# The first of two expert mixtures: sums kept in PSUM, weight splits moved to other steps, two output tiles interleaved

## The chip, the core and the metric

One core of a Trainium2 chip runs the whole program. Its engines work side by side and meet through semaphores: TensorE (PE in the profile, with its weight loads as PEld), VectorE (DVE), ScalarE (ACT), GpSimd (POOL), and SyncE (SP), whose queue issues most DMA transfers. TensorE writes its results into PSUM; everything else lies in SBUF. The metric is the device time of one execution in microseconds, lower is better.

## The reference

Attention with a cluster mask gives 1536 rows of 512 numbers. A first mixture of experts gives each row to exactly one of 8 experts, 192 rows to each. A second mixture runs all rows through all 4 experts and adds the results with given weights.

```python
def _moe_ref(x, w_gate, w1, w2):                 # x (1536, 512), 8 experts, F = 1024
    cap = N // E                                 # 192 rows per expert
    ...
    for e in range(E):
        mask = assigned == e
        h = np.maximum(x[mask] @ w1[e], 0.0)     # layer 1: 512 -> 1024
        out[mask] = h @ w2[e]                    # layer 2: 1024 -> 512

def _moe2_ref(x, domain_probs, w1, w2):          # 4 experts, every row through each
    for e in range(E):
        h = np.maximum(x @ w1[e], 0.0)
        out += p[:, e:e + 1] * (h @ w2[e])
```

## The kernel before

The program has four parts, one after the other: attention, routing (which rows belong to which expert), the first mixture and the second. All of the change lies in the function `moe`, nearly all of it in the first mixture. The order of the instructions on each engine is the order in which the code writes them; nothing reorders them.

**Numbers in halves.** Products are taken in a reduced fp32 format. So each operand is held as a high part and a low part (the rest), and the product is the sum of high times high, high times low and low times high. For weights, `split(l, e, i)` makes one chunk of 128x1024 of layer `l`, expert `e`: ScalarE copies `raw` to `hi` (line L1025), then GpSimd (first mixture, `i` even) or VectorE (all others) computes `lo = raw - hi` (L1026), and the next chunk's load goes to SP's queue. Each layer of an expert has four chunks. The pools `wp` hold four chunks of each kind, the ring of loaded chunks eight.

**One expert of the first mixture.** Its 192 rows lie transposed, high and low part beside each other, in `X1`. Layer 1 makes eight tiles `f`, each from four pairs of matmuls (L1129 with 384 columns: high and low rows times high weights; L1130 with 192 columns: high rows times low weights, added into the first half). Then come the transposes of the rows of a later expert (`fetch`, L1072), then layer 2 makes four tiles `i`, each from eight pairs (L1143, L1144) that read `h[:, k]`, the eight results of layer 1. A tile is one PSUM buffer `p` of a pool of six (name `p1`) and has two halves `p[:, 0]` and `p[:, 1]` that must be added.

**The join of a tile.** ScalarE copies the second half to SBUF (`r`, L1099), VectorE adds it to the first (`t`, L1100). One tile later (`later`, `flush`) ScalarE makes the high part from `t` (`h` or `XH`, L1104) and VectorE the low part (`h` at L1106, `XL` at L1108), which reads `t` and the high part. The last tile of layer 1 is joined to its end at once.

**Where the splits stand before.** In layer 1: for the first expert the last two chunks of its own layer 2 (tiles 0 and 1); for all, chunk 0 and 1 of the next expert's layer 1 behind tiles 3 and 5. In layer 2: two chunks each behind tiles 0 and 1, one each behind tiles 2 and 3.

**The second mixture** takes 512 rows at a time, layer 1 in eight tiles (L1164 to L1166), layer 2 in four (L1186 to L1188), with its own splits behind every second tile of some blocks.

Of the kernel before, what the change touches and what calls it, by code (L numbers as in the profile page):

```python
# [27 lines left out]
F32 = mybir.dt.float32  # L28
# [949 lines left out]
def moe(ctx, tc, xd, idx, w1, w2, u1, u2, out, idf, idb, route):  # L978

    nc = tc.nc  # L980
# [4 lines left out]
    cap = N // E1  # L985
    KD, KF = D // 128, F // 128
# [5 lines left out]
    XH = big.tile([128, KD, N], F32R, name="XH")  # L992
    XL = big.tile([128, KD, N], F32R, name="XL")
# [4 lines left out]
    for e in range(E1):  # L998
        a = w1[e].rearrange("(k p) f -> p k f", p=128)
        b = w2[e].rearrange("(k p) d -> p k d", p=128)  # L1000
        chunks += [(1, e, i, a[:, :, i * 256:(i + 1) * 256]) for i in range(4)]
        chunks += [(2, e, i, b[:, :, i * 128:(i + 1) * 128]) for i in range(4)]
    for e in range(E2):
        a = u1[e].rearrange("(k p) f -> p k f", p=128)
        b = u2[e].rearrange("(k p) d -> p k d", p=128)
        chunks += [(1, E1 + e, i, a[:, :, i * 256:(i + 1) * 256]) for i in range(4)]
        chunks += [(2, E1 + e, i, b[:, 2 * i:2 * i + 2, :]) for i in range(4)]
    raw, HI, LO, nload = {}, {}, {}, [0]

    def load():  # L1010
        if nload[0] < len(chunks):
            l, e, i, ap = chunks[nload[0]]
            t = ring.tile([128, 1024], F32, name="raw")
            nc.sync.dma_start(t.rearrange("p (a b) -> p a b", a=ap.shape[1]), ap)
            raw[l, e, i] = t
            nload[0] += 1

    def split(l, e, i, sub=None):

        if e == E1 + E2:  # L1020
            return
        w = raw.pop((l, e, i))
        hi = wp.tile([128, 1024], F32R, name=f"hi{l}")
        lo = wp.tile([128, 1024], F32R, name=f"lo{l}")
        nc.scalar.activation(hi, w, AF.Copy)  # L1025
        (sub or (nc.gpsimd if e < E1 and i % 2 == 0 else nc.vector)).tensor_sub(lo, w, hi)  # L1026
        HI[l, e, i], LO[l, e, i] = hi, lo
        load()
# [9 lines left out]
    with ExitStack() as mc:  # L1038
        xgp = mc.enter_context(tc.tile_pool(name="xgp", bufs=4))

        def gather(j):
            if j not in XG:
                XG[j] = xgp.tile([128, D + E2], F32, name="xg")
            nc.gpsimd.indirect_dma_start(out=XG[j], out_offset=None, in_=xd,
                                         in_offset=bass.IndirectOffsetOnAxis(ap=idx[:, j:j + 1], axis=0))

        def first_rows():
            for j in range(4):
                gather(j)

        route(first_rows, ahead)
        m1 = mc.enter_context(tc.tile_pool(name="m1", bufs=1))
        m2 = mc.enter_context(tc.tile_pool(name="m1b", bufs=2))
        pg = ctx.enter_context(tc.tile_pool(name="pg", bufs=6, space=bass.MemoryType.PSUM))
        pxt = ctx.enter_context(tc.tile_pool(name="pxt", bufs=2, space=bass.MemoryType.PSUM))


        wt = pg.tile([128, 4, 128], F32, name="p1")
        for _ in range(WARM):
            nc.tensor.matmul(wt, idb, idb[:, None, :].to_broadcast([128, 4, 128]), start=True, stop=True)  # L1060

        def xpose(j):

            x = XG.pop(j)
            parts = 2 if j < 2 else 1
            K = KD // parts
            ps = []
            for i in range(parts):
                p = (pg if parts > 1 else pxt).tile([128, K, 128], F32, name="p1" if parts > 1 else "px")
                for k in range(K):  # L1070
                    o = (i * K + k) * 128
                    nc.tensor.transpose(p[:, k], x[:, o:o + 128], idf)  # L1072
                ps.append(p)
            s = j * 128
            while s < (j + 1) * 128:
                e = s // cap
                z = min((e + 1) * cap, (j + 1) * 128)
                if e not in X1:
                    X1[e] = m1.tile([128, KD, 2, cap], F32R, name="X1", bufs=3)
                d = slice(s - e * cap, z - e * cap)  # L1080
                c = slice(s - j * 128, z - j * 128)
                for i, p in enumerate(ps):
                    t = X1[e][:, i * K:i * K + K]
                    nc.scalar.activation(t[:, :, 0, d], p[:, :, c], AF.Copy)
                    nc.vector.tensor_sub(t[:, :, 1, d], p[:, :, c], t[:, :, 0, d])
                s = z
            nc.gpsimd.tensor_copy(P[:, j], x[:, D:D + E2])

        later = []

        def flush():
            while later:
                later.pop(0)()

        def join(p, hi, lo, relu):

            r = m2.tile([128, cap], F32, name="r", bufs=3)
            t = m2.tile([128, cap], F32, name="t", bufs=3)
            nc.scalar.activation(r, p[:, 1], AF.Copy)  # L1099
            nc.vector.tensor_add(t, p[:, 0], r)  # L1100
            flush()

            def rest():
                nc.scalar.activation(hi, t, AF.Relu if relu else AF.Copy)  # L1104
                if relu:
                    nc.vector.scalar_tensor_tensor(lo, t, 0.0, hi, op0=OP.max, op1=OP.subtract)  # L1106
                else:
                    nc.vector.tensor_sub(lo, t, hi)  # L1108
            later.append(rest)

        done = [0]

        def fetch(n):
            while done[0] * 128 < min(n, N):
                xpose(done[0])
                if done[0] + 4 < NT:
                    gather(done[0] + 4)
                done[0] += 1

        for e in range(E1):  # L1120
            if e == 0:
                fetch(cap)
            h = m2.tile([128, KF, 2, cap], F32R, name="h")
            for f in range(KF):
                wh, wl = (t[1, e, f // 2].rearrange("p (a b) -> p a b", a=KD)[:, :, (f % 2) * 128:(f % 2) * 128 + 128]
                          for t in (HI, LO))
                p = pg.tile([128, 2, cap], F32, name="p1")
                for k in range(KD):
                    nc.tensor.matmul(p, wh[:, k], X1[e][:, k], start=(k == 0), stop=False)  # L1129
                    nc.tensor.matmul(p[:, 0], wl[:, k], X1[e][:, k, 0], start=False, stop=(k == KD - 1))  # L1130
                join(p, h[:, f, 0], h[:, f, 1], True)
                if f == KF - 1:
                    flush()
                if e == 0 and f < 2:
                    split(2, 0, 2 + f)
                if f in (3, 5):
                    split(1, e + 1, f // 2 - 1)
            fetch((e + 2) * cap)
            for i in range(KD):
                wh, wl = (t[2, e, i].rearrange("p (a b) -> p a b", a=KF) for t in (HI, LO))  # L1140
                p = pg.tile([128, 2, cap], F32, name="p1")
                for k in range(KF):
                    nc.tensor.matmul(p, wh[:, k], h[:, k], start=(k == 0), stop=False)  # L1143
                    nc.tensor.matmul(p[:, 0], wl[:, k], h[:, k, 0], start=False, stop=(k == KF - 1))  # L1144
                sl = slice(e * cap, (e + 1) * cap)
                join(p, XH[:, i, sl], XL[:, i, sl], False)
                if i < 2:
                    split(1, e + 1, 2 + i)
                split(2, e + 1, i)
        flush()  # L1150

    m2p = ctx.enter_context(tc.tile_pool(name="m2p", bufs=1))
# [2 lines left out]
    for e in range(E2):  # L1155
        for b in range(NB):
            bs = slice(b * 512, b * 512 + 512)
            hh, hl = [], []
            for f in range(KF):
                wh, wl = (t[1, E1 + e, f // 2].rearrange("p (a b) -> p a b", a=KD)[:, :, (f % 2) * 128:(f % 2) * 128 + 128]  # L1160
                          for t in (HI, LO))
                p = pg.tile([128, 512], F32, name="p1")
                for k in range(KD):
                    nc.tensor.matmul(p, wh[:, k], XH[:, k, bs], start=(k == 0), stop=False)  # L1164
                    nc.tensor.matmul(p, wh[:, k], XL[:, k, bs], start=False, stop=False)  # L1165
                    nc.tensor.matmul(p, wl[:, k], XH[:, k, bs], start=False, stop=(k == KD - 1))  # L1166
                a = hp.tile([128, 512], F32R, name="hh")
                c = hp.tile([128, 512], F32R, name="hl")
                nc.scalar.activation(a, p, AF.Relu)  # L1169
                nc.vector.scalar_tensor_tensor(c, p, 0.0, a, op0=OP.max, op1=OP.subtract)  # L1170
                hh.append(a), hl.append(c)
                if f % 2 and b == 0 and e:
                    split(2, E1 + e, f // 2)
                if f % 2 and b == NB - 1:
                    split(1, E1 + e + 1, f // 2)
            for s in range(4):
# [4 lines left out]
                for d in range(0, D, w):  # L1181
                    p = pg.tile([128, w], F32, name="p1")
# [94 lines left out]
```

## Time and profile before

| | |
|---|---|
| time, median of 3 runs | 1047.84 us (1047.08 to 1049.1) |
| profiled execution, its own time | 1047.87 us |
| its span in the trace | 1046.2 us |
| first mixture, first matmul of layer 1 to first matmul of the second mixture | 333.21 to 515.56 us |
| TensorE busy, share of the span | 1001.5 us, 96% |
| VectorE, ScalarE, GpSimd | 560.6, 434.1, 234.9 us |

The trace starts with the first instruction; all positions are microseconds from there. [...]

### The profile page before, as it was taken

How to read it: one execution, taken by the hardware profiler on the slowest of the kernel's cores; microseconds unless marked ns; L12 is line 12 of the kernel's file. 1: busy time of each engine (PE TensorE's matmuls, PEld its weight loads, DVE VectorE, ACT ScalarE, POOL GpSimd, SP SyncE). 2: the span in 40 equal slices, each digit the busy share in tenths (PEclk: the TensorE clock that was granted, in tenths of full speed). 3: DMA queues.
4: the chain of work that ended last, by engine and by line, in shares of the span. 5: the costliest groups of instructions: out<-in, count | busy, mean ns of one | idle time of the engine just before them, and what ended most of it. 6: DMA issues, size and time to landing. Idle time of an engine off the chain costs nothing.

```text
span 1046.2 us, 14208 instructions
## 1 busy us (share of the span) xinstructions
PE 1001.5 (96%) x5409; PEld 858.7 (82%) x5409; DVE 560.6 (54%) x1064; ACT 434.1 (41%) x911; POOL 234.9 (22%) x190
## 2 busy tenths in 40 slices
PE   8899999999978989898999999999999999999997
PEld 4699999899945988898888888888888888888886
DVE  7998898999884787787721141321413213142121
ACT  5777887778732666675611030210302103021010
POOL 5663453420053455454000000000000000001101
PEclk8999999999978999899999999999999999999999
DMA  7754354110093767556700010200102000000001
GB/s 191 177 127 102 89 139 119 47 39 24 11 310 89 209 185 214 175 182 186 237 0 1 1 61 21 81 1 1 61 21 81 1 1 1 1 11 31 21 21 40
DMA packets 80103, 86.43 MB, mean 83 GB/s; under 512 B 7200, under 2 KB 67104, under 8 KB 79776
## 3 DMA queue, kind: packets, MB, share of 16 engines
q1 hardware_dynamic: 78112, 79.17, 26.8%
q0 software_dynamic: 1920, 6.32, 1.9%
q8 instruction: 44, 0.72, 0.3%
q14 instruction: 27, 0.22, 0.1%
HBM read 69.32 MB, written 6.32 MB: 72 GB/s over the span
## 4 chain that ended last, share of the span: by engine, by line
PE 57%; issue 5%; DVE 4%; ACT 2%; DMA 0%; POOLq 0%; ACTq 0%; DVEq 0%
PE p L1164 8%; PE p L1165 8%; PE p L1166 8%; PE p L1187 8%; PE p L1186 8%; PE p L1188 8%; PE p L1143 3%; PE p L1129 2%; DVE lo L1026 1%; PE p L1144 1%; ACT hi L1025 1%; DVE t L1100 1%; PE p L1130 1%; DVE h L1106 1%; ACT r L1099 1%
## 5 line engine op out<-in xcount | busy, mean ns | idle before, releaser
L1169 ACT ACTIVATE hh<-p 128x512 fp32r<-128x512 f32 x96 | 57.4, 598 | 421.3 <-PE p L1166 419.9
L1170 DVE SCALAR_TENSOR_TENSOR hl<-p,hh 128x512 fp32r<-128x512 f32 x96 | 66.4, 692 | 172.3 <-ACT hh L1169 172.3
L1187 PE MATMUL p<-lo,hh 128*128 128x512 f32 (+1 forms) x392 | 152.6, 389 | 0.0
L1186 PE MATMUL p<-hi,hh 128*128 128x512 f32 (+1 forms) x392 | 151.9, 387 | 0.0
L1188 PE MATMUL p<-hi,hl 128*128 128x512 f32 (+1 forms) x392 | 150.4, 384 | 0.0
L1164 PE MATMUL p<-XH,hi 128*128 128x512 f32 x384 | 149.4, 389 | 0.0
L1165 PE MATMUL p<-XL,hi 128*128 128x512 f32 x384 | 149.4, 389 | 0.0
L1166 PE MATMUL p<-XH,lo 128*128 128x512 f32 x384 | 149.4, 389 | 0.0
L1195 POOL DMA_INDIRECT out_dram<-acc,idx x12 | 11.7, 973 | 532.8 <-DVE acc L1193 532.8
L1026 POOL TENSOR_TENSOR lo<-raw,hi 128x1024 fp32r<-128x1024 f32 x35 | 88.0, 2529 | 113.7 <-ACT hi L1025 70.2
L1193 DVE SCALAR_TENSOR_TENSOR acc<-p,P,acc 128x512 f32<-128x512 f32 (+1 forms) x37 | 27.3, 737 | 157.9 <-PE p L1188 157.9
L400 DVE TENSOR_TENSOR PL<-pT,PH 128x384 fp32r<-128x384 f32 x192 | 97.6, 549 | 7.4 <-ACT PH L399 4.4
L1025 ACT ACTIVATE hi<-raw 128x1024 fp32r<-128x1024 f32 x96 | 99.1, 1051 | 3.9 <-issue 2.9
L1143 PE MATMUL p<-h,hi 128*128 128x384 f32 x256 | 87.7, 402 | 13.2 <-DVE h L1106 13.2
L375 DVE TENSOR_REDUCE nm<-S 128x1 f32<-128x768 f32 x96 | 91.4, 953 | 16.5 <-PE S L373 15.8
L1026 DVE TENSOR_TENSOR lo<-raw,hi 128x1024 fp32r<-128x1024 f32 x61 | 90.2, 1490 | 11.3 <-ACT hi L1025 11.3
L399 ACT ACTIVATE PH<-pT 128x384 fp32r<-128x384 f32 x192 | 84.3, 492 | 28.6 <-PE pT L397 26.9
L383 ACT ACTIVATE e<-S,nm 128x768 f32<-128x768 f32 x96 | 86.7, 903 | 6.3 <-DVE nm L375 6.2
L1186 PEld LDWEIGHTS p<-hi,hh 128*128 128x128 f32 x392 | 73.6, 188 | 16.5
L1188 PEld LDWEIGHTS p<-hi,hl 128*128 128x128 f32 x392 | 73.6, 188 | 15.8
L1187 PEld LDWEIGHTS p<-lo,hh 128*128 128x128 f32 x392 | 73.7, 188 | 14.1
L1164 PEld LDWEIGHTS p<-XH,hi 128*128 128x128 f32 x384 | 72.1, 188 | 15.0
(271 smaller groups left out, 1856.1 us busy)
## 6 DMA issues: line engine op xcount, KB each, us to landing
raw<-in_moe_w_dram SPq DMA_DIRECT2D x96, 512.0 KB, 4.6
k<-in_k_dram SPq DMA_DIRECT2D x30, 192.0 KB, 3.8
q<-in_q_dram SPq DMA_DIRECT2D x30, 192.0 KB, 3.9
xd<-xs SPq DMA_DIRECT2D x2, 1548.0 KB, 5.9
vr<-in_v_dram SPq DMA_DIRECT2D x16, 192.0 KB, 2.6
KB<-KA SPq DMA_DIRECT2D x15, 192.0 KB, 3.6
M<-KA SPq DMA_DIRECT2D x14, 192.0 KB, 4.1
M<-QB SPq DMA_DIRECT2D x14, 192.0 KB, 3.7
```

The costliest lines, as they stand in the source:

```text
L375: nc.vector.tensor_reduce(nm, s, op=OP.max, axis=AX.X, negate=True)
L383: nc.scalar.activation(e, ST.pop(u), AF.Exp, bias=NM.pop(u), accum_out=SM[n][:, i:i + 1])
L400: nc.vector.tensor_sub(lo, p, hi)
L1025: nc.scalar.activation(hi, w, AF.Copy)
L1026: (sub or (nc.gpsimd if e < E1 and i % 2 == 0 else nc.vector)).tensor_sub(lo, w, hi)
L1143: nc.tensor.matmul(p, wh[:, k], h[:, k], start=(k == 0), stop=False)
L1164: nc.tensor.matmul(p, wh[:, k], XH[:, k, bs], start=(k == 0), stop=False)
L1165: nc.tensor.matmul(p, wh[:, k], XL[:, k, bs], start=False, stop=False)
L1166: nc.tensor.matmul(p, wl[:, k], XH[:, k, bs], start=False, stop=(k == KD - 1))
L1186: nc.tensor.matmul(p, hh[f][:, c], vh, start=(f == 0), stop=False)
L1187: nc.tensor.matmul(p, hh[f][:, c], vl, start=False, stop=False)
L1188: nc.tensor.matmul(p, hl[f][:, c], vh, start=False, stop=(f == KF - 1))
```

## The change

Three edits in the first mixture, and one line in the second that follows from them.

- The sum `t` of a tile's halves is no longer an SBUF tile; VectorE writes it back over the first half of the PSUM buffer, and the two later steps read it there.
- The splits stand elsewhere: layer 1 has one behind tiles 0, 1, 2 and 4, layer 2 one behind each of its four tiles. The last two chunks of an expert's layer 2 are now split in its own layer 1. For the second mixture's first expert they move into the second mixture (behind tiles 5 and 7 of its first block).
- Layer 2 takes tiles 0 and 1 together: steps 0 to 5 of tile 0, steps 0 to 5 of tile 1, steps 6 and 7 of tile 0, steps 6 and 7 of tile 1.

```diff
         def join(p, hi, lo, relu):
             r = m2.tile([128, cap], F32, name="r", bufs=3)
-            t = m2.tile([128, cap], F32, name="t", bufs=3)
+            t = p[:, 0]
             nc.scalar.activation(r, p[:, 1], AF.Copy)
-            nc.vector.tensor_add(t, p[:, 0], r)
+            nc.vector.tensor_add(t, t, r)
             flush()
...
-                if e == 0 and f < 2:
-                    split(2, 0, 2 + f)
-                if f in (3, 5):
+                if f < 2:
+                    split(2, e, 2 + f)
+                if f in (2, 4):
                     split(1, e + 1, f // 2 - 1)
             fetch((e + 2) * cap)
+            ps = {}
+            def second(i, ks):
+                if i not in ps:
+                    ps[i] = pg.tile([128, 2, cap], F32, name="p1")
+                wh, wl = (t[2, e, i].rearrange("p (a b) -> p a b", a=KF) for t in (HI, LO))
+                for k in ks:
+                    nc.tensor.matmul(ps[i], wh[:, k], h[:, k], start=(k == 0), stop=False)
+                    nc.tensor.matmul(ps[i][:, 0], wl[:, k], h[:, k, 0], start=False, stop=(k == KF - 1))
+            second(0, range(KF - 2))
+            second(1, range(KF - 2))
+            second(0, range(KF - 2, KF))
+            second(1, range(KF - 2, KF))
             for i in range(KD):
...
+                if i > 1:
+                    second(i, range(KF))
                 sl = slice(e * cap, (e + 1) * cap)
-                join(p, XH[:, i, sl], XL[:, i, sl], False)
+                join(ps[i], XH[:, i, sl], XL[:, i, sl], False)
                 if i < 2:
                     split(1, e + 1, 2 + i)
-                split(2, e + 1, i)
+                else:
+                    split(2, e + 1, i - 2)
...
-                if f % 2 and b == 0 and e:
+                if f % 2 and b == 0 and (e or f > KF // 2):
                     split(2, E1 + e, f // 2)
```

How this moves instructions is seen at two places. The first is ScalarE behind layer 2 of the first expert, from its tile 0 to its tile 3 (`r` and `XH` are the joins, `hi` the weight splits; the numbers tell buffers apart). Before:

```order
L1099 ACTIVATE r<-p_6840 128x192
L1025 ACTIVATE hi_6861<-raw 128x1024
L1025 ACTIVATE hi_6867<-raw 128x1024
L1099 ACTIVATE r<-p_6873 128x192
L1104 ACTIVATE XH<-t 128x192
L1025 ACTIVATE hi_6896<-raw 128x1024
L1025 ACTIVATE hi_6902<-raw 128x1024
L1099 ACTIVATE r<-p_6908 128x192
L1104 ACTIVATE XH<-t 128x192
L1025 ACTIVATE hi_6931<-raw 128x1024
L1099 ACTIVATE r<-p_6937 128x192
```

Of the change, the same place:

```order
L1099 ACTIVATE r<-p_6832 128x192
L1025 ACTIVATE hi_6869<-raw 128x1024
L1099 ACTIVATE r<-p_6845 128x192
L1104 ACTIVATE XH<-p_6832 128x192
L1025 ACTIVATE hi_6880<-raw 128x1024
L1099 ACTIVATE r<-p_6886 128x192
L1104 ACTIVATE XH<-p_6845 128x192
L1025 ACTIVATE hi_6908<-raw 128x1024
L1099 ACTIVATE r<-p_6914 128x192
L1104 ACTIVATE XH<-p_6886 128x192
L1025 ACTIVATE hi_6936<-raw 128x1024
```

Two pairs of splits became single ones, and `XH` reads the PSUM buffer in place of `t`. The second place is VectorE from the end of that layer 2 into layer 1 of the next expert (`lo` are the splits that VectorE does itself). Before:

```order
L1026 TENSOR_TENSOR lo_6897<-raw,hi_6896 128x1024
L1026 TENSOR_TENSOR lo_6903<-raw,hi_6902 128x1024
L1100 TENSOR_TENSOR t<-p_6908,r 128x192
L1108 TENSOR_TENSOR XL<-t,XH 128x192
L1100 TENSOR_TENSOR t<-p_6937,r 128x192
L1108 TENSOR_TENSOR XL<-t,XH 128x192
L1026 TENSOR_TENSOR lo_6961<-raw,hi_6960 128x1024
L1100 TENSOR_TENSOR t<-p_6967,r 128x192
L1108 TENSOR_TENSOR XL<-t,XH 128x192
L1100 TENSOR_TENSOR t<-p_6982,r 128x192
L1106 SCALAR_TENSOR_TENSOR h<-t,h 128x192
```

Of the change:

```order
L1026 TENSOR_TENSOR lo_6881<-raw,hi_6880 128x1024
L1100 TENSOR_TENSOR p_6886<-p_6886,r 128x192
L1108 TENSOR_TENSOR XL<-p_6845,XH 128x192
L1100 TENSOR_TENSOR p_6914<-p_6914,r 128x192
L1108 TENSOR_TENSOR XL<-p_6886,XH 128x192
L1026 TENSOR_TENSOR lo_6937<-raw,hi_6936 128x1024
L1100 TENSOR_TENSOR p_6943<-p_6943,r 128x192
L1108 TENSOR_TENSOR XL<-p_6914,XH 128x192
L1100 TENSOR_TENSOR p_6963<-p_6963,r 128x192
L1106 SCALAR_TENSOR_TENSOR h<-p_6943,h 128x192
L1026 TENSOR_TENSOR lo_6978<-raw,hi_6977 128x1024
```

Of the two splits in a row one has left layer 2, and one stands now behind tile 1 of layer 1; the steps `XL` and `h` read one SBUF operand and one in PSUM, where they read two in SBUF.

## Rows read from the trace of the kernel before

**Rows 1.** The page: granted TensorE clock in 40 slices of the span.

```profile
PEclk8999999999978999899999999999999999999999
```

**Rows 2.** Windows, one per expert (fifth, sixth), all eight summed, then the second mixture.

```profile
core 0: us, PE busy (x) PEld busy (x) DVE busy (x) ACT busy (x) POOL busy (x), PEclk, DMA share, GB/s
...
423.80:449.74 25.94, 22.71 (x134) 21.48 (x133) 19.81 (x32) 15.12 (x34) 11.24 (x7) 0.87 0.63 189
449.74:469.81 20.07, 19.80 (x139) 19.11 (x137) 16.89 (x30) 15.02 (x35) 9.52 (x6) 1.00 0.59 178
...
sum 182.35, PE 167.47 PEld 159.57 DVE 144.41 ACT 120.23 POOL 84.78; mean PE 20.93 PEld 19.95 DVE 18.05 ACT 15.03 POOL 10.60
...
530.00:1036.00 506.00, 506.00 (x2228) 417.22 (x2227) 128.40 (x163) 77.20 (x116) 9.74 (x10) 1.00 0.07 22
```

**Rows 3.** Windows, the longest of five stretches at half clock, and their sum.

```profile
438.43:445.25 6.82, 6.12 (x23) 6.06 (x24) 2.59 (x8) 3.43 (x6) 2.75 (x2) 0.50 0.39 128
...
sum 20.48, PE 19.77 PEld 19.36 DVE 8.78 ACT 13.07 POOL 5.22; mean PE 3.95 PEld 3.87 DVE 1.76 ACT 2.61 POOL 1.04
```

**Rows 4.** Timeline of PE, last expert: start, duration, what, idle before it.

```profile
495.03 0.36 PE L1129 MATMUL p<-X,hi 128*128 128x384 f32 x1
...
504.20 0.36 PE L1143 MATMUL p<-h,hi 128*128 128x384 f32 x1
...
507.31 0.45 PE L1143 MATMUL p<-h,hi 128*128 128x384 f32 x1 [1.51 <-DVE h L1106]
```

**Rows 5.** Timeline of PE, first expert's start of layer 2, and the second's transposes.

```profile
342.37 0.60 PE L1072 MATMUL px<-idf,xg 128*128 128x128 f32 x4
342.72 0.42 PE L1143 MATMUL p<-h,hi 128*128 128x384 f32 x1
...
346.28 0.69 PE L1143 MATMUL p<-h,hi 128*128 128x384 f32 x1 [1.13 <-DVE h L1106]
...
347.46 0.57 PE L1143 MATMUL p<-h,hi 128*128 128x384 f32 x1
...
347.99 0.57 PE L1143 MATMUL p<-h,hi 128*128 128x384 f32 x1
...
364.84 1.03 PE L1072 MATMUL px<-idf,xg 128*128 128x128 f32 x8
365.63 0.42 PE L1143 MATMUL p<-h,hi 128*128 128x384 f32 x1
```

**Rows 6.** Timelines of POOL, DVE and ACT in that stretch of the first expert.

```profile
341.40 2.40 POOL L1026 TENSOR_TENSOR lo<-raw,hi 128x1024 fp32r<-128x1024 f32 x1 [3.05 <-ACT hi L1025]
...
341.85 2.17 DVE L1106 SCALAR_TENSOR_TENSOR h<-t,h 128x192 fp32r<-128x192 f32 x1
...
344.47 1.21 DVE L1026 TENSOR_TENSOR lo<-raw,hi 128x1024 fp32r<-128x1024 f32 x1
345.61 0.35 DVE L1100 TENSOR_TENSOR t<-p,r 128x192 f32<-128x192 f32 x1
345.88 0.34 DVE L1106 SCALAR_TENSOR_TENSOR h<-t,h 128x192 fp32r<-128x192 f32 x1
...
342.23 1.05 ACT L1025 ACTIVATE hi<-raw 128x1024 fp32r<-128x1024 f32 x1
```

**Rows 7.** Instructions by line, whole program: count, then ns minimum/median/maximum, first and last start.

```profile
L1100 DVE TENSOR_TENSOR t<-p,r x96: 343/348/359, 335.0 to 517.1; 128x192 f32<-128x192 f32 x96
...
L1106 DVE SCALAR_TENSOR_TENSOR h<-t,h x64: 340/346/2174, 336.4 to 507.9; 128x192 fp32r<-128x192 f32 x64
...
L1108 DVE TENSOR_TENSOR XL<-t,XH x32: 341/348/2344, 352.0 to 518.7; 128x192 fp32r<-128x192 f32 x32
...
L1026 DVE TENSOR_TENSOR lo<-raw,hi x61: 1210/1226/3427, 338.5 to 932.8; 128x1024 fp32r<-128x1024 f32 x61
...
L1026 POOL TENSOR_TENSOR lo<-raw,hi x35: 2332/2397/3413, 295.7 to 494.7; 128x1024 fp32r<-128x1024 f32 x35
...
L1104 ACT ACTIVATE h<-t x64: 351/364/371, 336.0 to 507.6; 128x192 fp32r<-128x192 f32 x64
```

More of the change, by code (lines that the diff above doesn't have):

```diff
@@ L1133, in moe @@
                     flush()
-                if e == 0 and f < 2:
-                    split(2, 0, 2 + f)
-                if f in (3, 5):
+                if f < 2:
+                    split(2, e, 2 + f)
+                if f in (2, 4):
                     split(1, e + 1, f // 2 - 1)
             fetch((e + 2) * cap)
-            for i in range(KD):
[L1140 to L1144, printed above, removed]
+            ps = {}
[10 more added lines that the diff above has]
+            second(1, range(KF - 2, KF))
+            for i in range(KD):
+                if i > 1:
+                    second(i, range(KF))
                 sl = slice(e * cap, (e + 1) * cap)
-                join(p, XH[:, i, sl], XL[:, i, sl], False)
+                join(ps[i], XH[:, i, sl], XL[:, i, sl], False)
                 if i < 2:
                     split(1, e + 1, 2 + i)
-                split(2, e + 1, i)
+                else:
+                    split(2, e + 1, i - 2)
         flush()
```

## The prediction

> **What bounds the kernel now.** I looked first at where TensorE is not at full speed. The page's clock line [rows 1] shows the second half of the span at 9, and the window over the second mixture has TensorE busy for 506.00 of 506.00 us at clock 1.00 [rows 2]: nothing to gain there, and the change leaves its matmuls alone. The clock line dips in the slices of the first mixture. So that stretch, 333.21 to 515.56 us, is cut into one window per expert [rows 2]: the same work took 25.94 us at clock 0.87 for the fifth and 20.07 at 1.00 for the sixth, 182.35 us all eight together.
>
> How long should they take? Layer 1 of the last expert ran without a gap: 495.03 to 504.20, that is 9.17 us for 32 pairs of matmuls, 0.2865 us a pair [rows 4]. Layer 2 is 32 pairs of the same sizes, so an expert needs 18.34 us and eight need 146.7. The transposes add, start to start, 0.35 us where there are four and 0.79 where there are eight [rows 5]; four experts have four, three have eight, the last none, 3.8 us in all. Without any wait at full clock the stage takes 150.5 us. **31.9 us are lost.**
>
> They are lost in two ways. Five stretches, 20.48 us together, ran at half clock [rows 3]. There a pair took 0.53 us (347.46 to 347.99, [rows 5]) against 0.2865, so 0.46 of that time, 9.5 us, is the clock's price. The other 22.4 us are waits, and the timeline says for what: step 5 of layer 2's first tile waits 1.13 us for `h` in the first expert [rows 5], step 4 waits 1.51 us in the last [rows 4]. The releaser is VectorE's L1106 each time. The half clock begins right at such a wait (346.27 in the first expert, with the matmul that starts at 346.28 after its idle time); I take it as the wait's consequence.
>
> Why is `h` late? In the same stretch GpSimd's split runs from 341.40 for 2.40 us, and VectorE's L1106, begun at 341.85, takes 2.17 us and ends as GpSimd ends [rows 6]; its median is 0.346 us [rows 7]. `XL` (L1108) has a maximum of 2.344 us against 0.348. But L1100 never took more than 0.359 us in 96 runs [rows 7]. What tells them apart: L1106 and L1108 read two SBUF operands, L1100 one from PSUM and one from SBUF. So I read the rows as: a VectorE instruction with two SBUF operands waits until a running GpSimd split is done, one with a PSUM operand doesn't. VectorE's own splits (two SBUF operands) show the same, 3.427 us at most against 1.226 [rows 7].
>
> **The change, part by part.**
>
> *Sum in PSUM.* L1106 and L1108 now have the operand form that L1100 has. 96 of them lose the chance of a 2 us block. GpSimd's splits stay (four per expert), so they then block only VectorE's own splits. The new thing is VectorE writing its sum into PSUM; no row shows such a write. Below, I bound it by L1100 as it is (0.348 us, nothing added), above by twice that, 0.70. I take 0.35, since the row has the same operation, size and inputs. ScalarE then reads `t` from PSUM; its read of `t` from SBUF is 0.364 us [rows 7] and I leave it so.
>
> [...]
>
> The price of the edit itself is a PSUM buffer held longer: until the low part is made, a tile later. Six buffers, one tile per 1.146 us, so tile f+6 of layer 1 may not start before tile f's join is complete. The walk below says how close that comes.
>
> *Splits spread.* Their number and the loads' stay, two on VectorE and two on GpSimd in either layer, with loads still eight chunks ahead. What goes is two splits in a row on VectorE behind layer 2's tile 1. The last two chunks of the second mixture's first expert are split beside its layer 1, where VectorE is busy for 128 of 506 us [rows 2]: nothing.
>
> *Tiles 0 and 1 together.* `h` of tile 6 was wanted 6 pairs, 1.72 us, after layer 2's start; now 12 pairs, 3.44 us.
>
> **The walk.** A steady expert, time 0 at its layer 1's start; tile f ends at 1.146(f+1). I queue the instructions in the new order. On VectorE one join step follows the next after 0.27 us (345.61 to 345.88) and a split takes 1.14 (344.47 to 345.61, [rows 6]); on ScalarE a split takes about 1.0 (1.05 us, [rows 6]) and on GpSimd 2.4; a step on another engine starts when the one before it is done, some 0.35 us [rows 7]. The tile that ended at 0 is joined and split by ScalarE until 1.7, GpSimd's split of the tile before it holds VectorE's until 2.0, so that one ends at 3.1. Tile 0 is added then, made high by 4.0, and ScalarE splits behind tile 1 until 4.9. GpSimd's next split runs 3.3 to 5.7 and holds VectorE's till then, which so ends at 6.8. Tiles 2 and 3 are joined behind it, up to 8.4. The split behind tile 4 runs 9.1 to 10.25, with GpSimd done at 8.7. Then come `h` of tile 4 (ready 10.9), 5 (11.5), 6 (12.0) and 7 (12.5). Layer 2 starts at 9.52 (four transposes), 9.96 (eight) or 9.17 (none). It wants tile 4 after 1.15 us and tile 5 after 1.43. With four transposes it waits 0.5 us in all, with eight 0.1, with none 0.85; tiles 6 and 7, wanted at 13 or later, are there. The first expert has no backlog, so I give it 0.3, an estimate between these. Buffers: tile 7 would start at 8.0 and wants tile 1's, free at 7.45; 0.6 us to spare.
>
> **Sum.** Waits left: 3 x 0.5 + 3 x 0.1 + 0.85 + 0.3, about 3 us. No half clock: the sixth expert kept clock 1.00 [rows 2] with 0.9 us of waits (20.07 less 18.34 and 0.79). Stage 150.5 + 3 = 153.5 us, 28.9 less than 182.35. The profiled execution took 1047.87 us, span 1046.2; the median of the runs is 1047.84, so no correction: **1019.0 us**.
>
> **Rivals.**
>
> *The stalls are only halved.* VectorE's splits still meet GpSimd's (3.4 us), and a PSUM write of 0.70 us would put five more times 0.35, 1.75 us, onto `h` of tiles 4 and 5. Against: in the walk they meet once per expert, early. Then half of the experts wait 2 us more and fall to half clock for one stretch (20.48 / 6 is 3.4 us, 0.46 of it 1.6): 4 x 3.6 = 14.4 us, 1033 us.
>
> *Nothing is gained.* The stalls move: what `h` no longer waits, VectorE's own splits do, with as many clock dips. For it: those splits are 1.2 us each and block everything behind them. Against: before, one expert took 2 us blocks of both kinds, now only one kind is left. 1048 us.
>
> *Slower, by PSUM buffers.* The buffer is held through the join. If the steps that read `t` in PSUM still wait for GpSimd, two blocks of 2.1 us per layer 1 stand between a tile and its buffer. TensorE then stops inside layer 1 as well. It decides once VectorE runs 0.6 + 28.9 / 8 = 4.2 us later than walked, which is those two blocks. With three late tiles of 0.5 us more in each expert the time is 1048 + 12 = 1060 us. Against: L1100's maximum of 0.359 us.
>
> **Chances.** Forecast as summed (1015.5 to 1024) 0.75; halved 0.15; nothing gained 0.04; slower 0.06. The low end is the stage without any wait, 1047.87 - 31.9 = 1016.0, less a little for run to run. The high end goes to 1031: that takes in 1.4 us of waits more per expert, about a PSUM write at 0.70 us, and leaves out some 0.18. A measurement of this kernel can tell 0.2% (2 us) from no change: faster 0.90, same 0.04, slower 0.06.
>
> **What would show it.** Right: L1106 and L1108 with maxima under 0.4 us; TensorE's wait for `h` at steps 4 or 5 of tile 0 alone and under 1 us; clock 1.00 in all expert windows, each 18.4 to 20 us; VectorE's sum at 0.35 us. Wrong: any 2 us step of L1106 beside a GpSimd split; TensorE idle inside layer 1 for VectorE; a half-clock stretch between the first layer 2 and the second mixture; the sum's row at 0.5 us or more.

## The result and the profile after

The changed kernel took 1017.54 us (median of 4 runs, 1016.85 to 1020.62) beside 1048.18 us for the kernel before: a ratio of 0.9714, 95% interval 0.9692 to 0.9736, 30.6 us less. The forecast was 1019.0 us. The profiled execution took 1017.49 us with a span of 1015.8.

The page's clock line (PEclk, the granted TensorE clock in tenths of full speed), to be read against [rows 1]; each digit is a slice of 25.4 us:

```profile
PEclk9899999999997999999999999999999999999999
```

The dips in the slices of the first mixture are gone; the 7 is the slice from 304.7 to 330.1 us, ahead of it. The windows of the new experts, cut from first matmul to first matmul as before (first, second, fifth and last expert, then all eight, and a stretch of the second mixture) run from start to start, since listed durations overlap: behind a matmul that starts at 474.19 us and is listed with 0.36, the next starts at 474.39:

```profile
core 0: us, PE busy (x) PEld busy (x) DVE busy (x) ACT busy (x) POOL busy (x), PEclk, DMA share, GB/s
332.17:350.85 18.68, 18.68 (x132) 18.68 (x133) 12.56 (x27) 13.08 (x31) 12.08 (x9) 1.00 0.52 156
350.85:369.91 19.06, 19.06 (x138) 19.06 (x137) 14.84 (x32) 14.96 (x35) 13.40 (x9) 1.00 0.83 249
...
408.00:426.98 18.98, 18.98 (x135) 18.73 (x133) 14.07 (x30) 14.31 (x33) 11.26 (x6) 1.00 0.76 223
...
465.09:485.19 20.10, 18.70 (x131) 18.24 (x129) 15.31 (x33) 13.85 (x32) 4.65 (x2) 1.00 0.71 226
sum 153.02, PE 151.62 PEld 150.35 DVE 114.71 ACT 114.77 POOL 89.68; mean PE 18.95 PEld 18.79 DVE 14.34 ACT 14.35 POOL 11.21
...
500.00:1000.00 500.00, 500.00 (x2197) 412.11 (x2196) 129.77 (x164) 79.08 (x117) 8.78 (x9) 1.00 0.08 24
```

Against [rows 2] the stage fell from 182.35 to 153.02 us, 29.3 of the 30.4 us between the two spans; the remaining 1.1 us lie in the parts ahead of it (863.9 us outside the stage before, 862.8 after). The clock is 1.00 in all eight windows. VectorE's busy time in the stage went from 144.4 to 114.7 us with nearly the same instructions (one split fewer, one `XL` more): L1106 took 36.7 us in all before and 22.1 after, L1108 22.5 and 10.3, most of it time for which they had been held.

By line (count, then ns minimum/median/maximum), to be read against [rows 7]:

```profile
L1100 DVE TENSOR_TENSOR p<-p,r x96: 346/354/367, 333.9 to 486.1; 128x192 f32<-128x192 f32 x96
...
L1104 ACT ACTIVATE h<-p x64: 331/332/352, 335.0 to 477.7; 128x192 fp32r<-128x192 f32 x64
...
L1106 DVE SCALAR_TENSOR_TENSOR h<-p,h x64: 337/345/357, 335.4 to 478.0; 128x192 fp32r<-128x192 f32 x64
...
L1108 DVE TENSOR_TENSOR XL<-p,XH x32: 340/346/351, 347.8 to 488.1; 128x192 fp32r<-128x192 f32 x32
...
L1026 DVE TENSOR_TENSOR lo<-raw,hi x61: 1205/1227/2149, 336.3 to 902.4; 128x1024 fp32r<-128x1024 f32 x61
```

The maxima of L1106 and L1108 fell from 2174 and 2344 ns to 357 and 351. Their medians stayed. Only VectorE's own split, which still reads two SBUF operands, shows blocked runs (2149 ns at most against a median of 1227). This is not because the two kinds of step no longer meet a GpSimd split: before, 18 of the 96 steps of L1106 and L1108 began while one ran, and 16 of these took over 0.6 us; after the change 57 of 96 began so, and none did.

The waits in the stage (who waited, for whom: total us, times, longest) name one engine for which TensorE waited, VectorE. Before:

```profile
PEld p L1143 <- DVE h L1106: 20.0, 29, 1.7
...
PE p L1143 <- DVE h L1106: 13.2, 13, 1.5
...
PE p L1129 <- DVE t L1100: 1.6, 4, 0.5
```

Of the change:

```profile
PEld p L1147 <- DVE h L1106: 2.5, 5, 1.6
...
PE p L1147 <- DVE h L1106: 1.4, 1, 1.4
```

No row has L1129 (layer 1) waiting for VectorE any more; before, two experts waited there.

### The profile page after: what moved, and what is told of

The parts are those of the page before. It is cut to its first block, busy times and chain, and to the rows that moved or that the text cites. A ratio compares the mean times of both kernels' runs of the same rounds, so it can differ in the third digit from the quotient of the medians.

```text
span 1015.8 us, 14234 instructions
## 1 busy us (share of the span) xinstructions
PE 986.8 (97%) x5409; PEld 850.4 (84%) x5409; DVE 532.0 (52%) x1064; ACT 430.4 (42%) x911; POOL 239.7 (24%) x190
## 4 chain that ended last, share of the span: by engine, by line
PE 65%; issue 1%; ACT 0%; DVE 0%; DMA 0%; POOLq 0%; DVEq 0%; ACTq 0%
PE p L1177 9%; PE p L1179 9%; PE p L1178 9%; PE p L1200 9%; PE p L1199 9%; PE p L1201 8%; PE p L1147 5%; PE p L1129 4%; PE p L1148 2%; PE p L1130 2%; PE px L1072 0%; ACT hi L1025 0%; DMA out_dram<-acc,idx 0%; PE p L1072 0%; PE p L1060 0%
## 5 line engine op out<-in xcount | busy, mean ns | idle before, releaser
L1199 PE MATMUL p<-hi,hh 128*128 128x512 f32 (+1 forms) x392 | 151.9, 387 | 0.0
L1208 POOL DMA_INDIRECT out_dram<-acc,idx x12 | 11.7, 974 | 529.7 <-DVE acc L1206 529.7
L1025 ACT ACTIVATE hi<-raw 128x1024 fp32r<-128x1024 f32 x96 | 101.6, 1059 | 3.9 <-issue 2.9
L1026 DVE TENSOR_TENSOR lo<-raw,hi 128x1024 fp32r<-128x1024 f32 x61 | 88.0, 1443 | 24.1 <-ACT hi L1025 24.1
L1179 PEld LDWEIGHTS p<-XH,lo 128*128 128x128 f32 x384 | 72.1, 188 | 15.0
```

Source lines behind the costliest of these rows:

```text
L1199: nc.tensor.matmul(p, hh[f][:, c], vh, start=(f == 0), stop=False)
```

## The experiments

What had to be told apart: whether the sum in PSUM (call it part A) did the work by ending the blocks, with the spread splits (B) and the two tiles together (C) as small helpers, or whether one of these was the real gain. So each part was run alone and each was left out. Each ratio is against the kernel before, measured beside it on the same chip; a bracket behind a ratio is its 95% interval.

**A alone.**

```diff
-            t = m2.tile([128, cap], F32, name="t", bufs=3)
+            t = p[:, 0]
             nc.scalar.activation(r, p[:, 1], AF.Copy)
-            nc.vector.tensor_add(t, p[:, 0], r)
+            nc.vector.tensor_add(t, t, r)
```

> The kernel before with the sum kept in PSUM alone. Theory (the low-part steps waited for GpSimd's splits because they read two SBUF operands): L1106 and L1108 never above 0.4 us any more, and this part alone gives most of the 30.6 us: 1021 to 1027 us, with waits left inside layer 1 where two VectorE splits still stand in a row. Rival (the overlap of the two output tiles is what hides the wait): below 10 us gained, 1038 us or more, since layer 2 still wants h of the last tiles as early as before.

1036.98 us, ratio 0.9901 (0.9881 to 0.992): 11 us less, between the two expectations. The blocks are gone, as forecast. By line in this run:

```profile
L1106 DVE SCALAR_TENSOR_TENSOR h<-p,h x64: 340/348/358, 335.6 to 495.4; 128x192 fp32r<-128x192 f32 x64
...
L1108 DVE TENSOR_TENSOR XL<-p,XH x32: 341/344/350, 349.0 to 507.4; 128x192 fp32r<-128x192 f32 x32
```

What eats the rest is seen behind one layer 2, in the timelines of VectorE, GpSimd and TensorE:

```profile
391.68 0.35 DVE L1108 TENSOR_TENSOR XL<-p,XH 128x192 fp32r<-128x192 f32 x1
392.58 6.73 DVE L1026 TENSOR_TENSOR lo<-raw,hi 128x1024 fp32r<-128x1024 f32 x2 [0.55 <-ACT hi L1025]
399.23 0.35 DVE L1100 TENSOR_TENSOR p<-p,r 128x192 f32<-128x192 f32 x1
399.50 0.34 DVE L1108 TENSOR_TENSOR XL<-p,XH 128x192 fp32r<-128x192 f32 x1
...
390.12 8.10 POOL L1026 TENSOR_TENSOR lo<-raw,hi 128x1024 fp32r<-128x1024 f32 x3 [2.29 <-ACT hi L1025]
...
399.89 0.44 PE L1129 MATMUL p<-X,hi 128*128 128x384 f32 x1 [0.99 <-DVE XL L1108]
```

Three GpSimd splits run without a gap for 8.1 us, and the two VectorE splits in a row, which need 2.4 us when free, take 6.7 beside them. `XL` of layer 2's tile 1 stands behind them; with part A it is `XL` that frees the PSUM buffer, and tile 3 of the next layer 1 waits 0.99 us for it. So TensorE waited for a buffer in layer 1 of seven experts as well as for `h` in layer 2 of all eight, and the stage took 172.1 us.

**B alone.** Layer 1's splits behind tiles 0, 1, 2, 4 and one behind each tile of layer 2, all else as before:

```diff
-                if e == 0 and f < 2:
-                    split(2, 0, 2 + f)
-                if f in (3, 5):
+                if f < 2:
+                    split(2, e, 2 + f)
+                if f in (2, 4):
...
-                split(2, e + 1, i)
+                else:
+                    split(2, e + 1, i - 2)
...
```

> The kernel before with the splits spread alone. Theory: GpSimd's splits still block L1106 and L1108 for up to 2.2 us, now twice in layer 1; gain below 12 us, 1036 to 1046 us, and half-clock stretches stay. Rival (the two splits in a row were what made h late): at least 20 us gained, 1028 us or less.

1053.2 us, ratio 1.005 (1.0032 to 1.0068): slower, the sign of neither expectation. The blocks stay (L1106 up to 2443 ns; 22 of the 96 steps held, where 16 were), and two GpSimd splits now run in layer 1 where one did. TensorE waits for no other engine in layer 1, but in all eight experts it waits for `h`, and eight stretches, 27.3 us, run at half clock where five did.

**C alone.** Layer 2's first two tiles cut at step 6, splits and sum as before:

```diff
...
+            second(0, range(KF - 2))
+            second(1, range(KF - 2))
+            second(0, range(KF - 2, KF))
+            second(1, range(KF - 2, KF))
...
```

> The kernel before with layer 2's first two tiles taken together alone. Theory: the waits at steps 3 to 5 of the first tile stay, since these come before the second tile's cover; only what was waited at steps 6 and 7 goes, 8 x 0.5 us at most and perhaps a clock dip: 1040 to 1046 us. Rival (the cover is what counts): 1030 us or less.

1061.79 us, ratio 1.0126 (1.0108 to 1.0144): 13.7 us slower, against every expectation. (The profiled execution, from which the rows below come, was the longest of the four, 1066.67 us.) Tiles 0 and 1 now end 0.57 us apart, near the middle of layer 2, so the splits behind tile 0 start later and end closer to those behind tile 1. In VectorE's and TensorE's timelines at the change from the second to the third expert, whose layer 1 starts at 382.16:

```profile
380.05 1.23 DVE L1108 TENSOR_TENSOR XL<-t,XH 128x192 fp32r<-128x192 f32 x1
381.21 6.76 DVE L1026 TENSOR_TENSOR lo<-raw,hi 128x1024 fp32r<-128x1024 f32 x2
387.89 0.35 DVE L1100 TENSOR_TENSOR t<-p,r 128x192 f32<-128x192 f32 x1
...
388.30 0.44 PE L1129 MATMUL p<-X,hi 128*128 128x384 f32 x1 [1.42 <-DVE t L1100]
```

The 6.8 us of two blocked splits reach 5.8 us into layer 1, and its tile 4 waits for a buffer. These waits, total us and times, were there in two experts before and are in seven now:

```profile
PEld p L1129 <- DVE t L1100: 14.7, 14, 1.7
PE p L1129 <- DVE t L1100: 11.5, 14, 1.4
```

**Without A** (B and C).

```diff
-            t = p[:, 0]
+            t = m2.tile([128, cap], F32, name="t", bufs=3)
             nc.scalar.activation(r, p[:, 1], AF.Copy)
-            nc.vector.tensor_add(t, t, r)
+            nc.vector.tensor_add(t, p[:, 0], r)
```

> The changed kernel with the sum in SBUF again (spread splits and the two tiles together stay). Theory: L1106 and L1108 show 2 us runs beside GpSimd's splits again, half-clock stretches come back in some experts, 1028 to 1040 us. Rival (the other two parts are enough): 1022 us or less, clock 1.00 in the whole stage.

1061.14 us, ratio 1.0118 (1.0093 to 1.0143): the blocks and the half clock are back as the theory said, and dearer than its 1028 to 1040 us. By line:

```profile
L1106 DVE SCALAR_TENSOR_TENSOR h<-t,h x64: 340/350/2420, 336.8 to 519.8; 128x192 fp32r<-128x192 f32 x64
...
L1108 DVE TENSOR_TENSOR XL<-t,XH x32: 341/2176/2453, 352.9 to 532.4; 128x192 fp32r<-128x192 f32 x32
```

The median of L1108 is 2176 ns: spread out, GpSimd's splits held 21 of these 32 steps. This pair of edits needs A.

**Without B** (A and C).

```diff
-                if f < 2:
-                    split(2, e, 2 + f)
-                if f in (2, 4):
+                if e == 0 and f < 2:
+                    split(2, 0, 2 + f)
+                if f in (3, 5):
...
-                else:
-                    split(2, e + 1, i - 2)
+                split(2, e + 1, i)
...
```

> The changed kernel with the splits where they stood before (sum in PSUM and the two tiles together stay). Theory: layer 2's tile 1 has two VectorE splits in a row again, each up to 3.4 us beside GpSimd's, so some layer 1 waits for a PSUM buffer come back (before: 1.3 us in two experts) while h is in time: 1018 to 1023 us. Rival (spreading is needed for h too): 1027 us or more.

1034.94 us, ratio 0.9867 (0.9852 to 0.9882): the rival's number. By the ratios B is worth some 16 us to the changed kernel. The waits of this run's stage show both kinds:

```profile
PEld p L1129 <- DVE XL L1108: 11.2, 14, 1.0
...
PE p L1129 <- DVE XL L1108: 8.0, 14, 0.8
PEld p L1146 <- DVE h L1106: 7.2, 8, 1.9
PE p L1146 <- DVE h L1106: 5.4, 8, 1.7
```

Layer 1 waits for PSUM buffers in seven experts, and layer 2 for `h` in all eight. The clock stayed at 1.00.

**Without C** (A and B).

```diff
-            second(0, range(KF - 2))
-            second(1, range(KF - 2))
...
+                for k in range(KF):
+                    nc.tensor.matmul(p, wh[:, k], h[:, k], start=(k == 0), stop=False)
```

> The changed kernel with layer 2's tiles one after the other. Theory: VectorE leaves layer 1 with a backlog behind the split of tile 4, so h of tiles 4 to 7 arrives every 0.53 us while a pair takes 0.29: about 0.5 us more per expert than the changed kernel, 1020 to 1024 us, clock 1.00. Rival (without the cover the waits grow past what the clock stands): half-clock stretches in several experts, 1027 us or more.

1022.42 us, ratio 0.9762 (0.9745 to 0.9779): as the theory said. The stage took 156.5 us at clock 1.00, 3.5 more than with C, 0.4 per expert.

**Five PSUM buffers.**

```diff
-        pg = ctx.enter_context(tc.tile_pool(name="pg", bufs=6, space=bass.MemoryType.PSUM))
+        pg = ctx.enter_context(tc.tile_pool(name="pg", bufs=5, space=bass.MemoryType.PSUM))
```

> The changed kernel with five PSUM buffers in place of six. Theory (my walk: tile 1 of layer 1 is done with its buffer 0.6 us before tile 7 wants it): with five, tile 6 wants it 1.15 us earlier, so TensorE waits about 0.5 us inside layer 1 of seven experts, 3 to 6 us more than the changed kernel. Rival (buffers have much room): no difference, within 2 us. If the hold is worse than walked: 10 us or more.

1023.77 us, ratio 0.9773 (0.975 to 0.9795). That interval lies just above the changed kernel's first (0.9692 to 0.9736) and touches that of its second measurement below (0.9711 to 0.9752), so the trace decides. Layer 1 now waits for a buffer in seven experts, once in each and twice in the last (two pairs of 0.70 to 0.75 and 0.37 us where a pair takes 0.2865), 0.5 us each: the walk's spare 0.6 us less the 1.15 us of one buffer gave 0.55. `h` is then in time but for 0.8 us in the last expert, and the stage is 155.4 us, 2.4 more than with six.

**A alone with seven buffers** (and one, not two, for the transposes).

```diff
-        pg = ctx.enter_context(tc.tile_pool(name="pg", bufs=6, space=bass.MemoryType.PSUM))
-        pxt = ctx.enter_context(tc.tile_pool(name="pxt", bufs=2, space=bass.MemoryType.PSUM))
+        pg = ctx.enter_context(tc.tile_pool(name="pg", bufs=7, space=bass.MemoryType.PSUM))
+        pxt = ctx.enter_context(tc.tile_pool(name="pxt", bufs=1, space=bass.MemoryType.PSUM))
```

> The kernel before with the sum in PSUM alone, and seven PSUM buffers for tiles in place of six (the transposes keep one of two). That version with six waits 9.4 us inside layer 1 for buffers and took 1037 us. If the longer hold of the buffers is the cause, the waits go and the time falls by 7 us or more, 1030 or less. If the cause is VectorE's backlog behind the two splits in a row, the waits inside layer 1 shrink but layer 2 waits as much more for h: 1032 to 1037 us.

1054.86 us, ratio 1.0059 (1.0041 to 1.0077). The time settles nothing: with one buffer the second group of transposes waits for the first to be copied out, 5 us in each of three experts, and 20.6 us of the stage ran at half clock. Its waits still tell something:

```profile
PE px L1072 <- DVE X L1085: 15.1, 3, 5.1
...
PE p L1143 <- DVE h L1106: 6.8, 5, 2.0
...
PE p L1129 <- DVE XL L1108: 1.6, 5, 0.3
```

With six buffers the last two read 5.4 us (8 times) and 6.7 us (11 times). The waits for buffers nearly went, but those for `h` grew, which fits VectorE being as late as before and TensorE meeting it in layer 2. Whether all of A's missing gain is VectorE's backlog, and none the longer hold, this run doesn't settle.

**Cutting at step 4, and the last split a tile earlier.** The waits left stand at steps 4 and 5 of layer 2's tile 0:

```diff
-            second(0, range(KF - 2))
-            second(1, range(KF - 2))
-            second(0, range(KF - 2, KF))
-            second(1, range(KF - 2, KF))
+            second(0, range(KF - 4))
+            second(1, range(KF - 4))
+            second(0, range(KF - 4, KF))
+            second(1, range(KF - 4, KF))
```

> The changed kernel with layer 2's first two tiles cut at step 4 in place of step 6: steps 0 to 3 of tile 0, 0 to 3 of tile 1, then 4 to 7 of either. h of tile 4 is wanted 2.29 us after layer 2's start, not 1.15. Theory (what is left of the waits is at steps 4 and 5 of tile 0, about 2.8 us in the stage, most of it 1.9 us in the last expert): 2 to 2.8 us less than the changed kernel, no wait for h left. Rival (the wait only moves to tile 0's last steps): no difference.

Then again beside the changed kernel, with a version that has in addition

```diff
-                if f in (2, 4):
-                    split(1, e + 1, f // 2 - 1)
+                if f in (2, 3):
+                    split(1, e + 1, f - 2)
```

> The changed kernel itself once more, beside the others on one chip: 1016 to 1020 us, clock 1.00 from the first layer 2 on, some 2.5 us of waits for h, 1.9 of them in the last expert.

> Tiles 0 and 1 of layer 2 cut at step 4, a second time beside the changed kernel. Theory (waits left stand at steps 4 and 5 only): its stage is 1.5 to 2 us shorter, the time 1 to 2.5 us less than the changed kernel's beside it. Rival: within 0.5 us of it.

> Cut at step 4, and the last split of layer 1 behind tile 3 in place of tile 4, so that VectorE has one tile more to catch up before layer 2. Theory: the last expert's wait (1.2 us with the cut at 4) goes too; stage 150.2 to 150.8 us, time 2 to 3 us less than the changed kernel. Rival: two splits in a row behind tiles 2 and 3 hold VectorE longer and bring buffer waits of 0.5 us or more inside layer 1; no gain.

The changed kernel took 1019.13 us here (ratio 0.9731, 0.9711 to 0.9752), the cut at step 4 1018.42 (0.9709, 0.969 to 0.9728; the first time 1017.91, 0.9709), with the earlier split 1018.84 (0.9727, 0.9702 to 0.9752). The stage does get shorter: 153.1 us for the changed kernel, 151.4 with the cut at 4, 151.9 with the earlier split too. The second run of the cut has 154.06, but its trace shows the first expert's layer 1 at half clock up to 338.7 us, from a stretch that began ahead of the stage. A gain of 1 to 2 us is smaller than the runs tell apart. None of the three is shown to be the fastest.

## Why the prediction was right

**Where the time was lost.** The stage without waits was put at 150.5 us. The cut at step 4 reached 151.44, of which 1.2 us are waits in the last expert, so the bound holds to 0.3 us. 3 us of waits and a stage of 153.5 us were forecast, 153.02 was measured. The other 1.1 us by which the whole came out lower lie ahead of the stage and were not forecast. One product was slightly off: 0.46 of 20.48 us is 9.4 us, not 9.5.

**Why `h` was late.** VectorE's join steps with two SBUF operands were held when they began beside a GpSimd split (16 of 18, before), those with one operand in PSUM were not (0 of 57, after). In the kernel before, L1100, with one in PSUM, began beside a running split as often as L1106 and L1108 together, 18 times, and never took over 0.359 us. In the changed kernel and in A alone the maxima of L1106 and L1108 are near 0.36 us; B alone and B with C have up to 2.4, C alone 2.2. What this rests on is the changed operand; no run took GpSimd's splits away. By what mechanism the one waits for the other was not shown.

**The write into PSUM** was taken at 0.35 us between bounds of 0.35 and 0.70; it takes 0.354. A source in PSUM did not slow the two steps that now read it: the medians are 345 ns after and 346 before for L1106, 346 and 348 for L1108. ScalarE's read of `t` was left at 0.364 and fell to 0.332 with `t` in PSUM.

**Splits spread, given no price of its own.** The two chunks moved into the second mixture cost nothing, as forecast: from its first matmul to the end the span has 530.6 us before and after. In the sum the missing price did no harm, because the walk queued all three edits together in the new order, and no price of one edit entered it. But what I then expected of single edits was wrong. Alone, A gave 11 us, B lost 5, C lost 14; with A in place B gives 14 to 16 and, with both, C gives 3 to 5. A alone leaves two VectorE splits in a row that three GpSimd splits stretch to 6.7 us; B alone lets GpSimd block more join steps (22, where 16 were); C alone moves the stretched pair into the next layer 1. The gain of 30.6 us belongs to A and B together (25 to 26 us without C), not to a sum of three parts; without A no version was faster than the kernel before.

**Half clock as the wait's consequence.** The prediction read this from one stretch. Of the other four, one begins inside a wait for `h` and three begin 0.66 to 1.06 us after one; and the last expert waited 1.51 us [rows 4] and stayed at 1.00. In all versions with A and B the stage kept 1.00 after its first layer 1, the versions without A had 5 to 8 half-clock stretches, A alone one. That fits. But A and C without B waited up to 1.7 us in one go and had none in the stage, so which wait brings it on isn't settled, and no run took the wait away without changing something else.

**The waits left, expert by expert.** Start to start, experts with four transposes waited 0.3 us where 0.5 was forecast, those with eight and the first not at all (0.1 and 0.3). The last expert was mis-sized: 0.85 forecast, 1.8 measured (20.10 less 18.34; TensorE idle 1.40 us at step 4). So two of the signs named for a right forecast, a wait under 1 us and windows up to 20 us, were missed there, and it was in part luck that the stage came out within 0.5 us: 0.9 us too little in the last expert stood against 1.3 too much in the others. The walk gave its layer 1 two VectorE splits. It has three, since a chunk of the second mixture always goes to VectorE. VectorE's timeline there, and TensorE's matmul behind its wait:

```profile
470.05 1.75 DVE L1026 TENSOR_TENSOR lo<-raw,hi 128x1024 fp32r<-128x1024 f32 x1 [0.56 <-ACT hi L1025]
...
472.25 1.21 DVE L1026 TENSOR_TENSOR lo<-raw,hi 128x1024 fp32r<-128x1024 f32 x1
...
475.08 1.23 DVE L1026 TENSOR_TENSOR lo<-raw,hi 128x1024 fp32r<-128x1024 f32 x1 [0.56 <-ACT hi L1025]
...
476.49 0.35 DVE L1106 SCALAR_TENSOR_TENSOR h<-p,h 128x192 fp32r<-128x192 f32 x1
...
476.89 0.44 PE L1147 MATMUL p<-h,hi 128*128 128x384 f32 x1 [1.40 <-DVE h L1106]
```

The third split's 1.1 us are what the forecast lacked. The last VectorE row is `h` of tile 4: TensorE goes on at 476.89.

**The walk in a steady expert** came out within 0.4 us. In the sixth, from the start of its layer 1, VectorE's first two splits end at 3.3 and 6.7 us (3.1 and 6.8 walked), the one behind tile 4 at 10.1 (10.25), and `h` of tiles 4 to 7 at 10.6, 11.1, 11.7 and 12.2 (10.9, 11.5, 12.0 and 12.5). One reading beside it was wrong: VectorE's splits were said to meet GpSimd's once per expert (the walk itself has two such meetings). In this expert three of the four did, taking 1.53, 1.76 and 2.15 us in place of 1.23; TensorE did not wait all the same.

**Buffers.** 0.6 us to spare were walked; taking one buffer away gave waits of 0.5 us where 0.55 followed from the walk. The slower rival needed VectorE 4.2 us later, and that was not near.

## What to carry to other kernels

When VectorE steps show a long maximum beside a short median, compare their operands with those of a step that never does, and lay another engine's timeline beside them: here one operand in PSUM instead of SBUF took VectorE's critical steps out of GpSimd's way (357 ns at most after the change, up to 2344 before). These edits to the order of queued work could not be priced one by one: two of the three made the kernel slower alone, and the same two are worth some 15 and 4 us behind the first. So walk the queues once for the whole new order, and look for the expert or block that differs, here the last, whose work goes to another engine.

## What the runs showed of the hardware that was not expected

GpSimd was held beside VectorE too. In the changed kernel seven copies of 128x4 numbers on GpSimd (L1087) began some 0.06 us behind the start of a VectorE split and took 1.21 to 1.22 us, to about its end; the others, begun when no split ran or as one ended, took 0.18 to 0.20 us. ScalarE read 192 columns from PSUM in 0.332 us against 0.364 from SBUF: medians of the 64 `h` steps of L1104 after and before the change.
